# Fused attention and feed-forward: the local value product in fp32 without a split, its joined words in two buffers, and the global jobs at other steps

## The chip, the cores and the metric

The kernel runs on one core of one Trainium2 chip. The metric is the device time of one execution in microseconds; the number that counts is the median of several runs. The core's engines are named as in the profile: PE is TensorE (PEld its weight loads), DVE is VectorE, ACT is ScalarE, POOL is GpSimd, and SP is the engine that issues the transfers (its queue is SPq).

## The reference, cut to what matters

Eight batches of eight heads, 512 local and 32 global positions, head dimension 64. The attention result is laid out as 4608 tokens of 512 and goes through a feed-forward layer with a squared relu.

```
k_all = np.concatenate([k_g, k_l], axis=2)
v_all = np.concatenate([v_g, v_l], axis=2)
s_g = scale * np.matmul(q_g, k_all.transpose(0, 1, 3, 2))
out_g = np.matmul(sm(s_g), v_all)
s_ll = scale * np.matmul(q_l, k_l.transpose(0, 1, 3, 2))
mask = np.abs(pos[:, None] - pos[None, :]) <= window          # window = 32
s_ll = np.where(mask, s_ll, -1000000000.0)
s_lg = scale * np.matmul(q_l, k_g.transpose(0, 1, 3, 2))
a_l = sm(np.concatenate([s_lg, s_ll], axis=-1))
out_l = np.matmul(a_l, np.concatenate([v_g, v_l], axis=2))
...
h = np.maximum(x @ w_in, 0.0)
return (h * h @ w_out).astype(np.float32)
```

Global queries see all 544 keys; a local query sees the 32 global keys and the local keys at most 32 away.

## The kernel before, in words

**Units.** The work is cut into 128 "heads" t: a batch, a half of its 512 local positions (256 queries) and one of eight heads. Eight heads make a group; a group's 256 tokens are one block of the feed-forward layer, which is cut into eight steps m. There are 16 such blocks and a 17th for the global tokens: 136 steps. One loop (line 614) runs both: iteration t works on head t's scores and softmax, on head t−1's product with the values, and on feed-forward step m = t − 9. An iteration is called a step below.

**Precision.** The first 16 heads ("plain") use fp32 matmuls on the raw data. From head 16 on an operand is split into a head, the value rounded to fp32r by a cast on ACT, and a rest, the difference, by a subtraction on DVE; several fast matmuls (head by head, head by rest, rest by head) stand for one in fp32. So split_qk and split_qk_rest (lines 132 and 142) treat q and k, split_v (149) the values, parts and parts_rest (238, 243) the turned probabilities, act2 (495) the hidden values.

**One local head.** load_head (91) loads raw(t): 608 columns of k and q and 192 of values, 400 KB. split_qk takes the heads of q and k into the tile qk, split_qk_rest the rests. scores (155) multiplies into s. softmax1 (172) adds the mask and takes the maximum on DVE into prob, softmax2 (192) takes the exponentials and their sums on ACT, softmax3 (201) the reciprocal and the scaling on DVE. turn (223) copies prob on POOL into planes of 16-bit words and has a DMA transpose turn them into the tile turned; join (231) puts the words together again on POOL in the tile joined. av (250) multiplies with the values into xa, nine matmuls of 128 or 256 moving columns. x_evac (278) takes the result out as x_h and x_l, the operands of the feed-forward layer.

**The feed-forward step.** gemm1 (472), in two halves, multiplies x with the first weights into h; act1 (488) takes relu and square into the PSUM tile pt, act2 the split gh and gl; gemm2 (506), in two halves, adds into the two output tiles o, which evac (528) copies to ot and stores after eight steps.

**Global heads.** Four local heads share a global score tile (g_scores, line 313); its work is spread over later steps as jobs (lines 692 to 711), a step and a place in the step for each: g_load_v and g_split_v for the values, g_soft, g_exp and g_norm for the softmax, g_turn and g_join for the turning (POOL copies and a DMA transpose too), g_parts for the split, g_av for the product gxo (13 matmuls), g_x for the result.

**The order.** From iteration 17 on (FREE, line 33) instructions issued through pe, ve, ac, po and sp stay in the order of the program on their engine; SP's transfers issued through sp are among them: turn's transpose and the loads of raw. An engine executes its instructions in that order, so an instruction that waits holds back all that stand behind it. In one step of the kernel before ACT runs x_evac(t−2), split_v(t), softmax2(t), parts(t−1), split_qk(t+1), act1, act2; SP runs turn(t)'s transpose and then load_head(t+2).

```
        if live and not early:
            softmax3(t)
            turn(t)
        if NPLAIN <= t + 2 < NT:
            load_head(t + 2)
```

The whole code of the functions that the change touches:

Of the kernel before, what the change touches and what calls it, by code (L numbers as in the profile page):

```python
# [7 lines left out]
F32 = mybir.dt.float32  # L8
F32R = mybir.dt.float32r
# [7 lines left out]
DM, DFF = 512, 2048  # L17
P = 128
HALF = 256
NGR = 2 * B  # L20
NT = NGR * H
# [17 lines left out]
def f(ap):  # L39
    return ap.bitcast(F32)  # L40
# [19 lines left out]
def attention_moe(  # L60
# [30 lines left out]
    def load_head(t):  # L91
        if plain(t):
            w_take(1)
            raw = wp.tile([P, 1024], F32, tag="w", name=f"raw{t}")[:, :PK]
        else:
            raw = p2.tile([P, PS], F32, tag="raw", name=f"raw{t}")
        if t == 0:
            nc.sync.dma_start(raw[:, : QC + KC], pk[t, :, : QC + KC])
        else:
            sp.dma_start(raw, pk[t, :, : raw.shape[1]])  # L100
        heads[t] = dict(raw=raw)

    load_head(0)
    con = cp.tile([P, P + 4 * WIN], F32, name="con")
# [15 lines left out]
    prob = cp.tile([P, 2 * WIN], F32, name="prob")  # L120
    planes = cp.tile([P, 1024], U16, name="planes")
    turned = cp.tile([P, 8, P], U16, name="turned")
    joined = cp.tile([P, 512], F32, name="joined")
    ml = cp.tile([P, P], F32R, name="ml")
    nc.gpsimd.memset(planes, 0)
    nc.gpsimd.memset(f(ml), 0.0)
    pt = ps_a.tile([P, 512], F32, name="pt")
    nc.gpsimd.memset(f(qgz), 0.0)
    nc.gpsimd.memset(sg[:, :, 608:], 0.0)
# [12 lines left out]
    def split_qk_rest(t):  # L142
# [2 lines left out]
        raw, hi = heads[t]["raw"], heads[t]["hi"]  # L145
        ve.tensor_sub(hi[64:, :KC], raw[64:, :KC], f(hi[64:, :KC]))
        ve.tensor_sub(hi[:, QK:], raw[:, KC:QK], f(hi[:, KC:QK]))

    def split_v(t):
        raw = heads[t]["raw"]  # L150
        v = heads[t]["v"] = p2.tile([P, 2, 192], F32R, tag="v", name=f"v{t}")
        ac.copy(v[:, 0, :], raw[:, QK:])
        ve.tensor_sub(v[:, 1, :], raw[:, QK:], f(v[:, 0, :]))

    def scores(t):
        hd = heads[t]
# [72 lines left out]
        sp.dma_start_transpose(out=turned, in_=planes)  # L229

    def join(t):
        words = joined.bitcast(U16).rearrange("p (n h) -> p h n", h=2)
        po.tensor_copy(words, turned.rearrange("p (h c) n -> p h (c n)", h=2))

    def sides(z):
        return z.rearrange("p (c n) -> p c n", n=128)[:, 0:4:3, :]

    def parts(t):

        ph = heads[t]["ph"] = p1.tile([P, 512], F32R, tag="ph", name=f"ph{t}")  # L240
        ac.copy(ph, joined)

    def parts_rest(t):
        ph = heads[t]["ph"]
        pl = heads[t]["pl"] = p1.tile([P, 256], F32R, tag="pl", name=f"pl{t}")
        ve.tensor_sub(ph[96:, 128:384], joined[64:96, 128:384], f(ph[64:96, 128:384]))
        ve.tensor_sub(ml[:64, :], joined[:64, 192:320], f(ph[:64, 192:320]))
        ve.tensor_sub(pl.rearrange("p (c n) -> p c n", c=2), sides(joined), sides(f(ph)))

    def av(t):  # L250
        hd = heads[t]
        c = QC + KC
        if plain(t):

            xa = ps_a.tile([P, HALF], F32, tag="xa", name=f"xa{t}")
            v, pts = hd["raw"][:, c:], hd["pts"]
            mm = [
                (xa, v[:, 0:128], pts[:, 256:512]),
                (xa[:, 0:128], v[:, 64:192], pts[:, 0:128]),
                (xa[:, 128:256], v[:, 128:256], pts[:, 128:256]),  # L260
            ]
        else:
            xa = ps_a.tile([64, HALF], F32, tag="xa", name=f"xa{t}")
            v, ph, pl = hd["v"], hd["ph"], hd["pl"]
            mm = []
            for u in range(2):
                o, vs, hs = xa[:, 128 * u : 128 * u + 128], slice(64 * u, 64 * u + 64), slice(384 * u, 384 * u + 128)
                mm += [(o, v[:, 0, vs], ph[:, hs]), (o, v[:, 1, vs], ph[:, hs])]
            mm += [(xa, v[:, i, 128:], ph[:, 128:384]) for i in range(2)]
            mm.append((xa[:, 64:192], v[:, 0, 128:], ml))  # L270
            for u in range(2):
                o, vs, ps = xa[:, 128 * u : 128 * u + 128], slice(64 * u, 64 * u + 64), slice(128 * u, 128 * u + 128)
                mm.append((o, v[:, 0, vs], pl[:, ps]))
        for i, (o, a, b) in enumerate(mm):
            pe.matmul(o, a, b, start=i == 0, stop=i == len(mm) - 1, skip_group_check=True)
        hd["xa"] = xa[:64, :]
# [14 lines left out]
    def g_load(t):  # L291

        b, grp = t // 16, (t // 4) % 2

        def cols(z, j):
            return bass.AP(z.tensor, z.offset + 64 * j, [list(z.ap[0]), [256, 2], [160, 2], [1, 32]])

        src = qg[b, grp].rearrange("p (a b) n -> p a b n", a=2)
        if plain(t):
            qz = p1.tile([P, 512], F32, tag=("ph", "gvl", "gvh", "ph")[t // 4], name=f"qz{t}")  # L300
            nc.gpsimd.memset(qz, 0.0)
            qr = p1.tile([P, 2, 2, 32], F32, tag="qr", name=f"qr{t}")
            (nc.sync if t else nc.scalar).dma_start(qr, src)
            nc.gpsimd.tensor_copy(cols(qz, 0), qr)
        else:
            qz = qgz
            qr = p1.tile([P, 2, 2, 32], F32, tag="qr", name=f"qr{t}")
            nc.sync.dma_start(qr, src)
            ac.copy(cols(qgz, 0), qr)
            ve.tensor_sub(cols(qgz, 1), qr, f(cols(qgz, 0)))  # L310
        state["qz"] = qz
# [215 lines left out]

    def evac(blk, tiles=(0, 1)):
        for i in tiles:
            pool, tag = ((p1, "ptl"), (p1, "gvl"))[i]  # L530
            ot = pool.tile([P, DM], F32, tag=tag, name=f"ot{blk}_{i}")
            ac.copy(ot, moe["o"][i])
            if blk < NGR:
                b, hf = divmod(blk, 2)
                r0 = b * 544 + 32 + hf * 256 + i * P
                nc.sync.dma_start(out[r0 : r0 + P, :], ot)
            else:
                for bb in range(4):
                    r0 = (4 * i + bb) * 544
                    nc.sync.dma_start(out[r0 : r0 + 32, :], ot[32 * bb : 32 * bb + 32, :])  # L540
# [41 lines left out]
    def w_tick(t, place):  # L582
        if t < len(PLAN):
            for c in PLAN[t].split(",")[place]:
                {"b": w_pass, "s": w_chunk}[c]()
# [28 lines left out]
    for t in range(NSTEP + LAG + 1):  # L614
# [11 lines left out]
            transposes(t - 1)  # L626
        if new:
            join(t - 1)
        for job, *args in jobs.pop((t, 6), ()):
            job(*args)  # L630
        if live and not early:
            scores(t)
        if old:
            pt_copy(t - 1)
        if NPLAIN <= t - 2 < NT:
            x_evac(t - 2)
        done = 0 < m <= NSTEP and m % 8 == 1 and m > 8
        if done:
            evac(m // 8 - 1, (0,))
        if live:  # L640
            softmax1(t)
        if run:
            gemm1(m, 0)
        if live and not early:
            split_v(t)
        if live:
            softmax2(t)
        if new:
            parts(t - 1)
        if live and not early:  # L650
            softmax3(t)
            turn(t)
        if NPLAIN <= t + 2 < NT:
            load_head(t + 2)
        for place in (4, 3):
            for job, *args in jobs.pop((t, place), ()):
                job(*args)
        if done:
            evac(m // 8 - 1, (1,))
        w_tick(t, 0)  # L660
        if live and early:
            g_scores(t)
# [5 lines left out]
            g_scores(t)  # L668
        if early and t + 1 < NPLAIN:
            scores(t + 1)  # L670
        if t + 1 < NT and not early:
            split_qk(t + 1)
        if run:
            act1(m)
        if old:
# [4 lines left out]
        w_tick(t, 1)  # L680
        if t + 1 == NPLAIN:
            split_qk(t + 1)
        if new:
            parts_rest(t - 1)
        if t + 1 < NT:
            split_qk_rest(t + 1)
        if live:
# [2 lines left out]
            if t % 4 == 3 and t + 1 < NT:  # L690
                g_load(t + 1)
        if live and t % 4 == 3 and (t // 8) % 2 == 1:
            d = t if t % 8 == 3 else t + 2
            for at, *job in (
                (d, 2, g_load_v, 0),
                (d + 1, 3, g_soft),
                (d + 1, 1, g_exp),
                (d + 2, 3, g_norm),
                (d + 3, 3, g_split_v, 0),
                (d + 3, 2, g_load_v, 1),  # L700
                (d + 3, 6, g_turn),
                (d + 4, 6, g_join),
                (d + 4, 3, g_parts),
                (d + 4, 0, g_av, 0),
                (max(d + 5, 17), 3, g_x, 0),
                (d + 5, 2, g_split_v, 1),
                (max(d + 6, 17), 0, g_av, 1),
                (max(d + 7, 18), 3, g_x, 1),
            ):
                place, job, *args = job  # L710
                jobs.setdefault((at, place), []).append((job, t, *args))
        for job, *args in jobs.pop((t, 2), ()):
            job(*args)
        if m == NSTEP:
            for i in range(2):
# [2 lines left out]
                evac(NBLK - 1, (i,))  # L718
        elif m > 0:
            gemm2(m - 1, 0)  # L720
        for job, *args in jobs.pop((t, 0), ()):
            job(*args)
        if 0 < m < NSTEP:
            gemm2(m - 1, 1)
        if new:
            av(t - 1)
        if run:
            act2(m)
        w_tick(t, 2)
        for job, *args in jobs.pop((t, 1), ()):  # L730
            job(*args)
# [82 lines left out]
```

## Time and profile before

| | |
|---|---|
| median of 3 runs | 1070.35 us (1070.1 to 1071.05) |
| the profiled execution | 1071.19 us, of which 1069.1 us lie between its first and last instruction (the span) |
| mean granted TensorE clock | 0.994 |
| DMA queue of SP and ACT | 126.32 MB, 44.5% of the time of 16 DMA engines |

The profile is that of one execution. A page sums it up; the other views answer questions to its trace. In lists of groups stand: line, engine, operation, out<-in by the tile's names (numbers left out), shapes, how many; then busy microseconds and mean nanoseconds of one; then the idle time of the engine just before and what ended it. Nearly all instructions carry line 53, a helper's, so tiles tell them apart. In the list of waits stand: engine and tile, what it waited for, microseconds in all, how often, the longest. In a timeline: start, duration, engine, operation, how many in one row. Matmuls are pipelined, so one record overlaps the next; what a stream of them costs is read from start to start. One fp32 matmul leaves two records. In the list of transfers the last number is the time from issue to landing.

### The profile page before, as it was taken

How to read it: one execution, taken by the hardware profiler on the slowest of the kernel's cores; microseconds unless marked ns; L12 is line 12 of the kernel's file. 1: busy time of each engine (PE TensorE's matmuls, PEld its weight loads, DVE VectorE, ACT ScalarE, POOL GpSimd, SP SyncE). 2: the span in 40 equal slices, each digit the busy share in tenths (PEclk: the TensorE clock that was granted, in tenths of full speed). 3: DMA queues.
4: the chain of work that ended last, by engine and by line, in shares of the span. 5: the costliest groups of instructions: out<-in, count | busy, mean ns of one | idle time of the engine just before them, and what ended most of it. 6: DMA issues, size and time to landing. Idle time of an engine off the chain costs nothing.

```text
span 1069.1 us, 20564 instructions
## 1 busy us (share of the span) xinstructions
PE 1029.5 (96%) x7040; PEld 902.3 (84%) x7040; DVE 867.7 (81%) x2445; ACT 721.5 (67%) x1743; POOL 385.0 (36%) x544
## 2 busy tenths in 40 slices
PE   8999989999999999999999999999999999999998
PEld 6776778988898888888888889888888888889896
DVE  5689878899989888898979999898989999893311
ACT  6889766767767766767666766776667676664432
POOL 1010344444445343444444443453445353441000
PEclk9999989999999999999999999999999999999999
DMA  9772444445444544454544444545444454341000
GB/s 367 310 258 80 104 103 115 114 116 125 116 123 101 136 103 101 115 118 123 122 115 116 116 120 109 123 104 125 125 110 105 118 135 110 103 95 54 5 21 20
DMA packets 193576, 127.69 MB, mean 119 GB/s; under 512 B 143552, under 2 KB 168640, under 8 KB 193472
## 3 DMA queue, kind: packets, MB, share of 16 engines
q1 hardware_dynamic: 193328, 126.32, 44.5%
q8 instruction: 55, 0.90, 0.4%
q14 instruction: 49, 0.40, 0.1%
q10 hardware_dynamic: 144, 0.07, 0.0%
HBM read 82.84 MB, written 8.91 MB: 86 GB/s over the span
## 4 chain that ended last, share of the span: by engine, by line
PE 43%; DVE 37%; ACT 8%; issue 5%; DMA 3%; POOL 2%; SPq 0%; DVEq 0%; POOLq 0%; ACTq 0%
PE o L53 17%; PE h L53 16%; DVE prob L53 6%; DVE st L53 5%; DVE qk L53 5%; PE xa L53 4%; ACT prob L53 3%; DVE v L53 3%; PE s L53 3%; DVE gl L53 2%; PE gxo L53 2%; DVE x_l L53 2%; DVE ph L53 2%; DVE pl L53 2%; DMA raw<-in_pk_dram 2%
## 5 line engine op out<-in xcount | busy, mean ns | idle before, releaser
L53 PE MATMUL h<-x_h,ws 128*128 128x256 f32 x2048 | 391.4, 284 | 0.0
L53 PEld LDWEIGHTS h<-x_h,ws 128*128 128x128 f32 x2048 | 329.1, 192 | 0.7
L53 PE MATMUL o<-ws,gh 128*128 128x512 f32 x1024 | 324.4, 398 | 3.2 <-ACT ot L53 3.0
L53 PE MATMUL h<-x_l,ws 128*128 128x256 f32 x1024 | 290.9, 284 | 1.1 <-DVE x_l L53 1.1
L53 POOL COPY joined<-turned 128x1024 uint16<-128x1024 uint16 x112 | 155.3, 1387 | 378.1 <-DMA turned<-planes 232.9
L53 POOL COPY planes<-prob 128x448 uint16<-128x448 uint16 x336 | 171.3, 547 | 152.1 <-DVE prob L53 152.1
L53 PEld LDWEIGHTS o<-ws,gh 128*128 128x128 f32 x1024 | 182.5, 189 | 38.2 <-ACT ot L53 7.0
L53 PE MATMUL o<-ws,gl 128*128 128x512 f32 x512 | 202.1, 395 | 0.0
L53 PEld LDWEIGHTS h<-x_l,ws 128*128 128x128 f32 x1024 | 197.0, 192 | 3.2 <-DVE x_l L53 2.6
L53 ACT ACTIVATE prob<-prob,st 128x224 f32<-128x224 f32 x224 | 106.3, 475 | 90.3 <-DVE st L53 89.5
L53 DVE TENSOR_TENSOR gl<-pt,gh 128x512 fp32r<-128x512 f32 x128 | 87.5, 684 | 73.2 <-ACT gh L53 72.0
L53 DVE TENSOR_TENSOR qk<-raw,qk 64x352 fp32r<-64x352 f32 x224 | 109.1, 487 | 8.7 <-ACT qk L53 1.6
L53 PEld LDWEIGHTS o<-ws,gl 128*128 128x128 f32 x512 | 96.3, 188 | 23.1
L53 ACT ACTIVATE pt<-h 128x512 f32<-128x512 f32 x128 | 74.2, 580 | 54.3 <-PE h L53 54.0
L53 ACT CAST x_h<-xa 64x256 fp32r<-64x256 f32 x120 | 43.7, 364 | 98.2 <-PE xa L53 97.9
L53 ACT CAST ph<-joined 128x512 fp32r<-128x512 f32 x112 | 68.9, 615 | 41.2 <-POOL joined L53 39.0
L53 PE MATMUL s<-qk 128*128 128x224 f32 x448 | 83.5, 298 | 8.2 <-DVE qk L53 5.6
L53 DVE TENSOR_SCALAR st<-st 128x2 f32<-128x2 f32 x128 | 62.5, 488 | 34.0 <-ACT prob L53 29.8
L53 ACT CAST qk<-raw 128x608 fp32r<-128x608 f32 x112 | 78.1, 697 | 8.7 <-DMA raw<-in_pk_dram 8.6
L53 DVE TENSOR_TENSOR v<-raw,v 128x192 fp32r<-128x192 f32 x112 | 80.5, 719 | 0.0
L53 DVE CUSTOM_DVE_ANT_0 prob<-s,con 128x224 f32<-128x224 f32 x224 | 77.7, 382 | 3.0 <-PE s L53 1.3
L53 ACT ACTIVATE pt<-pt 128x512 f32<-128x512 f32 x128 | 74.5, 582 | 4.0
(85 smaller groups left out, 1616.9 us busy)
## 6 DMA issues: line engine op xcount, KB each, us to landing
raw<-in_pk_dram SPq DMA_DIRECT2D x112, 400.0 KB, 3.5
wr<-in_w_dram SPq DMA_DIRECT2D x32, 512.0 KB, 8.0
gv<-in_vg_dram SPq DMA_DIRECT2D x32, 320.0 KB, 3.8
out_dram<-ot SPq DMA_DIRECT2D x32, 256.0 KB, 2.4
raw<-in_pk_dram SPq DMA_DIRECT2D x15, 432.0 KB, 8.2
qr<-in_qg_dram SPq DMA_DIRECT2D x31, 64.0 KB, 3.1
turned<-planes SPq DMA_TRANSPOSE x112, 3.1
out_dram<-ot SPq DMA_DIRECT2D x8, 64.0 KB, 1.7
```

The costliest lines, as they stand in the source:

```text
L53: r = method(*args, **kwargs)
```

## The change

The local values and the turned probabilities are no longer split: av multiplies them as they are, in fp32, with three matmuls in place of nine. The functions split_v, parts and parts_rest and their tiles are gone. The values come by a load of their own (load_v, at the start of step t), so that raw holds 608 columns. joined becomes a tile with two buffers, and so does ot. In the loop, evac takes both tiles at one place, split_qk(t+1) stands between softmax1 and softmax2 (in steps with an evac behind softmax2), the jobs of place 6 (g_turn, g_join) stand behind turn, those of place 0 (g_av) ahead of gemm2's first half, av between gemm2's two halves, and x_evac at the end of the same step. The global jobs get another list of steps.

```diff
         else:
-            raw = p2.tile([P, PS], F32, tag="raw", name=f"raw{t}")
+            raw = p2.tile([P, QK], F32, tag="raw", name=f"raw{t}")
...
+    def load_v(t):
+        v = heads[t]["v"] = p2.tile([P, 192], F32, tag="v", name=f"v{t}")
+        sp.dma_start(v, pk[t, :, QK:PS])
...
-    joined = cp.tile([P, 512], F32, name="joined")
-    ml = cp.tile([P, P], F32R, name="ml")
...
-    def split_v(t):
...
     def join(t):
+        joined = heads[t]["pts"] = p2.tile([P, 512], F32, tag="joined", name=f"joined{t}")
         words = joined.bitcast(U16).rearrange("p (n h) -> p h n", h=2)
         po.tensor_copy(words, turned.rearrange("p (h c) n -> p h (c n)", h=2))
-
-    def sides(z):
...
-    def parts(t):
...
-    def parts_rest(t):
...
-            v, ph, pl = hd["v"], hd["ph"], hd["pl"]
...
+            v, pts = hd["v"], hd["pts"]
+            mm = [
+                (xa, v[:, 128:], pts[:, 128:384]),
+                (xa[:, 0:128], v[:, 0:64], pts[:, 0:128]),
+                (xa[:, 128:256], v[:, 64:128], pts[:, 384:512]),
+            ]
...
         for i in tiles:
-            pool, tag = ((p1, "ptl"), (p1, "gvl"))[i]
-            ot = pool.tile([P, DM], F32, tag=tag, name=f"ot{blk}_{i}")
+            ot = p2.tile([P, DM], F32, tag="ot", name=f"ot{blk}_{i}")
...
         if new:
             join(t - 1)
-        for job, *args in jobs.pop((t, 6), ()):
-            job(*args)
         if live and not early:
+            load_v(t)
             scores(t)
         if old:
             pt_copy(t - 1)
-        if NPLAIN <= t - 2 < NT:
-            x_evac(t - 2)
         done = 0 < m <= NSTEP and m % 8 == 1 and m > 8
         if done:
-            evac(m // 8 - 1, (0,))
+            evac(m // 8 - 1)
         if live:
             softmax1(t)
         if run:
             gemm1(m, 0)
-        if live and not early:
-            split_v(t)
+        if t + 1 < NT and not early and not done:
+            split_qk(t + 1)
         if live:
             softmax2(t)
-        if new:
-            parts(t - 1)
+        if t + 1 < NT and not early and done:
+            split_qk(t + 1)
         if live and not early:
             softmax3(t)
             turn(t)
+        for job, *args in jobs.pop((t, 6), ()):
+            job(*args)
         if NPLAIN <= t + 2 < NT:
             load_head(t + 2)
...
-        if done:
-            evac(m // 8 - 1, (1,))
         w_tick(t, 0)
...
-        if t + 1 < NT and not early:
-            split_qk(t + 1)
         if run:
             act1(m)
...
-        if new:
-            parts_rest(t - 1)
         if t + 1 < NT:
             split_qk_rest(t + 1)
...
-            d = t if t % 8 == 3 else t + 2
+            d = t if t % 8 == 3 else t + 1
             for at, *job in (
-                (d, 2, g_load_v, 0),
                 (d + 1, 3, g_soft),
                 (d + 1, 1, g_exp),
                 (d + 2, 3, g_norm),
-                (d + 3, 3, g_split_v, 0),
-                (d + 3, 2, g_load_v, 1),
+                (d + 2, 1, g_load_v, 0),
                 (d + 3, 6, g_turn),
                 (d + 4, 6, g_join),
-                (d + 4, 3, g_parts),
-                (d + 4, 0, g_av, 0),
-                (max(d + 5, 17), 3, g_x, 0),
-                (d + 5, 2, g_split_v, 1),
-                (max(d + 6, 17), 0, g_av, 1),
-                (max(d + 7, 18), 3, g_x, 1),
+                (d + 4, 3, g_split_v, 0),
+                (d + 4, 1, g_load_v, 1),
+                (d + 5, 3, g_parts),
+                (d + 6, 0, g_av, 0),
+                (d + 6, 1, g_split_v, 1),
+                (d + 6, 1, g_x, 0),
+                (d + 7, 0, g_av, 1),
+                (d + 7, 1, g_x, 1),
             ):
...
         elif m > 0:
             gemm2(m - 1, 0)
...
+        if new:
+            av(t - 1)
         if 0 < m < NSTEP:
             gemm2(m - 1, 1)
-        if new:
-            av(t - 1)
         if run:
             act2(m)
+        if new:
+            x_evac(t - 1)
```

More of the change, by code (lines that the diff above doesn't have):

```diff
@@ L122, in attention_moe @@
     turned = cp.tile([P, 8, P], U16, name="turned")
-    joined = cp.tile([P, 512], F32, name="joined")
-    ml = cp.tile([P, P], F32R, name="ml")
     nc.gpsimd.memset(planes, 0)
-    nc.gpsimd.memset(f(ml), 0.0)
     pt = ps_a.tile([P, 512], F32, name="pt")
@@ L147, in split_qk_rest @@
         ve.tensor_sub(hi[:, QK:], raw[:, KC:QK], f(hi[:, KC:QK]))
-    def split_v(t):
[L150 to L153, printed above, removed]
     def scores(t):
@@ L231, in join @@
     def join(t):
+        joined = heads[t]["pts"] = p2.tile([P, 512], F32, tag="joined", name=f"joined{t}")
         words = joined.bitcast(U16).rearrange("p (n h) -> p h n", h=2)
         po.tensor_copy(words, turned.rearrange("p (h c) n -> p h (c n)", h=2))
-    def sides(z):
-        return z.rearrange("p (c n) -> p c n", n=128)[:, 0:4:3, :]
-    def parts(t):
-        ph = heads[t]["ph"] = p1.tile([P, 512], F32R, tag="ph", name=f"ph{t}")
-        ac.copy(ph, joined)
-    def parts_rest(t):
[L244 to L248, printed above, removed]
     def av(t):
@@ L263, in av @@
             xa = ps_a.tile([64, HALF], F32, tag="xa", name=f"xa{t}")
-            v, ph, pl = hd["v"], hd["ph"], hd["pl"]
[L265 to L273, printed above, removed]
+            v, pts = hd["v"], hd["pts"]
[4 more added lines that the diff above has]
+            ]
         for i, (o, a, b) in enumerate(mm):
@@ L299, in g_load @@
         if plain(t):
-            qz = p1.tile([P, 512], F32, tag=("ph", "gvl", "gvh", "ph")[t // 4], name=f"qz{t}")
+            qz = p1.tile([P, 512], F32, tag=("ptl", "gvl", "gvh", "ptl")[t // 4], name=f"qz{t}")
             nc.gpsimd.memset(qz, 0.0)
@@ L652, in attention_moe @@
             turn(t)
+        for job, *args in jobs.pop((t, 6), ()):
+            job(*args)
         if NPLAIN <= t + 2 < NT:
             load_head(t + 2)
-        for place in (4, 3):
-            for job, *args in jobs.pop((t, place), ()):
-                job(*args)
-        if done:
-            evac(m // 8 - 1, (1,))
+        for job, *args in jobs.pop((t, 3), ()):
+            job(*args)
         w_tick(t, 0)
@@ L711, in attention_moe @@
                 jobs.setdefault((at, place), []).append((job, t, *args))
-        for job, *args in jobs.pop((t, 2), ()):
+        for job, *args in jobs.pop((t, 0), ()):
             job(*args)
@@ L720, in attention_moe @@
             gemm2(m - 1, 0)
-        for job, *args in jobs.pop((t, 0), ()):
-            job(*args)
+        if new:
+            av(t - 1)
         if 0 < m < NSTEP:
             gemm2(m - 1, 1)
-        if new:
-            av(t - 1)
         if run:
             act2(m)
+        if new:
+            x_evac(t - 1)
         w_tick(t, 2)
```

## Prediction

> **What bounds the kernel now.** I read the page first (busy time, chain), then the waits of the engines and of SP's queue, then the timeline of one step of the loop.
>
> ```profile
> span 1069.1 us, 20564 instructions
> ...
> PE 1029.5 (96%) x7040; PEld 902.3 (84%) x7040; DVE 867.7 (81%) x2445; ACT 721.5 (67%) x1743; POOL 385.0 (36%) x544
> ...
> PE 43%; DVE 37%; ACT 8%; issue 5%; DMA 3%; POOL 2%; SPq 0%; DVEq 0%; POOLq 0%; ACTq 0%
> ```
>
> ```profile
> PEld s L53 <- DVE qk L53: 16.7, 51, 2.0
> ...
> PEld gxo L53 <- DVE ptl L53: 11.3, 13, 0.9
> ...
> ACT qk L53 <- DMA raw<-in_pk_dram: 8.6, 7, 3.5
> ```
>
> TensorE is nearly full, and when it does stand, it is mostly VectorE that is late (the rests of q and k for the next scores, the rests for the global product). The third row matters below: already now the load of the next head's raw lands so late that ACT waits for it seven times, at the place where the split stands today. How much it stands is read from the step. The first and last scores of the local heads and the matmuls of one step:
>
> ```profile
> L53 PE MATMUL s<-qk x448: 269/274/665, 96.8 to 952.5; 128*128 128x224 f32 x150
> ```
>
> ```profile
> 541.85 2.88 PE h L53 x24
> ```
>
> ```profile
> 599.73 0.63 PE L53 MATMUL o<-ws,gh 128*128 128x512 f32 x2
> ...
> 601.13 0.63 PE L53 MATMUL xa<-ph,v 128*64 128x128 f32 x6
> ...
> 601.78 0.65 PE L53 MATMUL s<-qk 128*128 128x224 f32 x4
> 602.27 0.29 PE L53 MATMUL h<-x_h,ws 128*128 128x256 f32 x1
> ...
> 605.60 0.29 PE L53 MATMUL gs<-qk,qgz 128*128 128x288 f32 x1
> 605.73 0.62 PE L53 MATMUL o<-ws,gh 128*128 128x512 f32 x2
> ...
> 607.11 0.22 PE L53 MATMUL gxo<-gvh,pth 128*64 128x128 f32 x1
> ...
> 607.89 0.44 PE L53 MATMUL o<-ws,gh 128*128 128x512 f32 x1
> ```
>
> Matmuls overlap, so start to start is the price. 448 matmuls at four a head are 112 heads, 111 steps in 952.5 − 96.8 − 0.5 = 855 us: 7.70 us a step. Without waits a step is four s 0.49 (601.78 to 602.27), 24 h 2.88, one gs 0.13, twelve o 2 × 1.40 (599.73 to 601.13), nine xa 0.65: 6.95. The 28 global products in this stretch (13 matmuls, 607.11 to 607.89: 0.78) add 0.20 a step. So 0.55 a step, 61 us in all, is TensorE standing still.
>
> **The change: the product.** Nine split matmuls at 0.65 become three in fp32 over 256, 128 and 128 moving columns. The plain heads run just such a set:
>
> ```profile
> 89.58 1.04 PE L53 MATMUL xa<-pts,raw 128*128 128x256 f32 x6
> 90.46 1.88 PE L53 MATMUL o<-wf,r 128*128 128x512 f32 x4
> ```
>
> Six records, 0.88 start to start. There the stationary side has 128 columns and here 64, which can only make the weight loads shorter, and those run beside the matmuls; the bounds are the 0.65 of now, if fp32 cost nothing more, and the 1.04 to the end of the last record. I take 0.88, since start to start is how the other terms are counted. TensorE's step without waits grows by 0.23 to 7.18, 7.38 with the global products; over 111 steps +26 us if TensorE sets the pace. The Trainium skill (FP8 and Floating Point Precision, TensorE Precision Notes) counts four passes for true fp32. At four times the split price (h: 0.12 us for 256 columns) that would be 0.96 us; the row's 0.88 is a little less, and the measured row is used. By the rule this term would be 9 us larger.
>
> **What it removes.**
>
> ```profile
> L53 ACT CAST ph<-joined 128x512 fp32r<-128x512 f32 x112 | 68.9, 615 | 41.2 <-POOL joined L53 39.0
> L53 DVE TENSOR_TENSOR v<-raw,v 128x192 fp32r<-128x192 f32 x112 | 80.5, 719 | 0.0
> L53 DVE TENSOR_TENSOR ph<-joined,ph 32x256 fp32r<-32x256 f32 x112 | 63.0, 563 | 9.2 <-ACT ph L53 5.8
> ```
>
> These three alone are 0.62 us of ACT and 1.28 us of VectorE a step; the casts of v and the ml and pl rests go too. This is what would end most of the 61 us of waits, if nothing else came in.
>
> **What it moves: the point that decides.** split_qk(t+1), which reads raw(t+1), moves from behind gemm1's second half to ahead of softmax2(t) on ACT, in all steps but those with an eviction. And raw(t+2) is still issued on SP behind turn(t), which waits for the three copies to planes, which wait for softmax2(t). ACT and SP keep program order from step 17 on. So raw(t+1) → split → softmax2(t) → softmax3 → planes → transpose issue → raw(t+2) becomes a ring closed once per step. Before, the split stood behind the softmax, right ahead of act1, and the ring closed over two steps. Behind the waiting split on ACT now stand softmax2, act1, gh and x_h; for them wait VectorE (softmax3, gl, x_l), POOL with its copies, and TensorE, whose next scores need the rests of q and k that VectorE takes after softmax3. That SP does hold the load back, and how long the ring is:
>
> ```profile
> SPq L53 <- POOL planes L53: 439.8, 123, 6.2
> ```
>
> ```profile
> 604.24 0.48 ACT L53 ACTIVATE prob<-prob,st 128x224 f32<-128x224 f32 x1 [1.52 <-DVE st L53]
> ...
> 604.43 0.35 DVE L53 TENSOR_TENSOR v<-raw,v 128x192 fp32r<-128x192 f32 x1
> ...
> 605.09 0.19 ACT L53 ACTIVATION_READ_ACCUMULATOR prob<-prob,st 128x1 f32 x1
> ...
> 605.69 0.70 ACT L53 CAST qk<-raw 128x608 fp32r<-128x608 f32 x1
> ...
> 606.19 1.78 POOL L53 COPY planes<-prob 128x448 uint16<-128x448 uint16 x3 [1.86 <-DVE prob L53]
> ...
> 607.99 1.24 SPq L53 DMA_TRANSPOSE turned<-planes  x1
> ...
> 609.32 0.53 SPq L53 DMA_DIRECT2D raw<-in_pk_dram  x1
> ```
>
> ```profile
> 613.49 1.19 POOL L53 COPY planes<-prob 128x448 uint16<-128x448 uint16 x3 [0.93 <-DVE prob L53]
> ```
>
> ```profile
> L53 POOL COPY joined<-turned 128x1024 uint16<-128x1024 uint16 x112 | 155.3, 1387 | 378.1 <-DMA turned<-planes 232.9
> ...
> raw<-in_pk_dram SPq DMA_DIRECT2D x112, 400.0 KB, 3.5
> ...
> turned<-planes SPq DMA_TRANSPOSE x112, 3.1
> ...
> raw<-in_pk_dram SPq DMA_DIRECT2D x1, 304.0 KB, 3.1
> ```
>
> raw's buffer was free when v's rest ended at 604.78, yet the load went out at 609.32, right behind the transpose: it is SP's order, not the buffer, that times it. The ring: split 0.70; the two exponentials with their sums 1.04 (604.24 to 605.28); reciprocal and scaling until the first copy 0.91 (to 606.19); the copies 1.19 to 1.78, taken as 1.70, since the q and k rests will run on VectorE beside them; to the transpose 0.02; transpose issue to load issue 1.33; landing 3.1 to 3.5, taken as 3.3, since the load shrinks from 400 to 304 KB, the size of the page's other row. Sum 9.0 us, against 7.38 for TensorE and 7.70 now. TensorE is not late in this ring: after scores it has 6.7 us of matmuls to do and waits for the rest of the 9.0, and the product finds its operand ready, as the join ends before the next raw lands (below). Nor are VectorE or ACT: what is left of their work, some 0.6 and 1.3 us a step less than now by the three rows above (on ACT the one, on VectorE the other two), fitted into 7.70.
>
> Two kinds of steps differ. In a step with an eviction (one in eight) softmax2 goes ahead of the split, and the copies wait only for the join before them on POOL. The transpose went out 1.33 before the load, so it has landed 1.33 + 3.3 − 3.1 = 1.5 before raw; the join (1.39) ends 0.1 before raw lands. The copies start there and not 0.70 + 1.04 + 0.91 = 2.65 after it: 2.8 us are saved, 0.35 a step. And g_turn, twice in 16 steps, now follows turn: its copies and its transpose come between turn's transpose and the load.
>
> ```profile
> L53 POOL COPY gp<-sg 128x1088 uint16<-128x1088 uint16 x16 | 19.2, 1198 | 30.3 <-ACT sg L53 30.3
> ...
> L53 POOL COPY gp<-sg 128x64 uint16<-128x64 uint16 x48 | 10.2, 249 | 0.0
> ```
>
> That is 1.20 + 3 × 0.25 = 1.95 of copies and some 1.4 for the issue in place of 1.33: +2.1, 0.26 a step. Period: 9.0 − 0.35 + 0.26 = 8.9 us. 111 × (8.9 − 7.70) = +133 us.
>
> Costed at nothing: the separate v load (one issue of half a microsecond, which stands ahead of turn on SP, in the time that SP waits for the copies anyway; without that cover 0.5 a step); the second buffers of joined and of the evicted tile; x_evac in the same step (TensorE's last six o, 1.40, cover it until the next gemm1); the spread of the global jobs (it takes away waits such as the 11.3 us above, which the ring would hide in any case). After the last head nothing changes. The profiled execution took 1071.19, 2.1 over its span; 1071.2 + 133 = 1204, and the median of the runs, 1070.35, lies 0.8 lower: **1203**. Bounds of the ring: copies 1.19 and landing 3.1 give 8.2 (1126); copies 1.78 and landing 3.5 give 9.2 (1237); landings are longer when other transfers run, so I keep room above.
>
> **Rivals.**
> *The ring does not close* (faster): the smaller raw goes out as soon as its buffer is free and has landed when ACT asks. It decides if the way from raw to raw is under 7.38, which needs the landing 1.6 us shorter than taken, or another order on SP. Then TensorE paces: 111 × 7.38 = 819, with a third of the 61 us of waits left 839, so 16 under 855: 1055. For it: VectorE loses work. Against: the SP row and 604.78 against 609.32. Chance 0.09.
> *Only the fp32 price* (slower): no ring, and the waits stay: +26, 1096. Against it: VectorE is relieved. Chance 0.04.
> *The ring and the clock* (much slower): TensorE now rests 8.9 − 7.18 = 1.7 us a step. Two rests of that length in a row did halve its clock once:
>
> ```profile
> 139.70 0.45 PE L53 MATMUL xa<-ph,v 128*64 128x256 f32 x2 [1.80 <-DVE ph L53]
> ...
> 142.52 1.44 PE L53 MATMUL s<-qk 128*128 128x224 f32 x4 [1.84 <-DVE qk L53]
> ```
>
> ```profile
> 142.00:148.00 6.00, 5.48 (x24) 5.31 (x25) 4.54 (x14) 5.01 (x12) 3.68 (x4) 0.50 0.37 116
> ```
>
> Six microseconds at clock 0.50 cost 3: such a step takes 7.38 + 3 = 10.4. Without a rest in it the clock comes back, so it would alternate with 8.9: mean 9.65, 1070 + 111 × 1.95 = 1287. Against: single rests, 7 us apart. Chance 0.08. The Trainium skill (TensorE: Matmul & The Clock Gate, the table of what matters for your kernels) only forbids rests over about 3 us; by it the clock would hold in ordinary steps.
>
> **How the numbers follow.** The ring as summed has 0.79, its own range 1140 to 1270. The rivals at 1055 and 1096 (0.13) are left out, the clock's is taken in part; range 1140 to 1270. This measurement can tell 0.2%, 2 us, from no change. Faster 0.08 (the first rival, but for a rest), same 0.02, slower 0.90.
>
> **What would show it.** Right: ACT qk waits for DMA raw in most steps (now 7 times), by 1.5 us and more; steps near 8.9; DVE far below 81%; TensorE waits for qk. The product at 0.88. Wrong: steps near 7.4 and no wait for raw.

## The result, and the profile after

The changed kernel takes **1215.08 us** (median of 4 runs, 1213.34 to 1216.68) beside 1070.7 us for the kernel before on the same chip: ratio 1.1349, 95% interval 1.1329 to 1.1368. It is slower, by 144 us.

The page of the changed kernel, busy time and then the chain that ended last:

```profile
span 1211.6 us, 19435 instructions
...
PE 1101.4 (91%) x6704; PEld 913.3 (75%) x6704; DVE 645.9 (53%) x1997; ACT 618.3 (51%) x1519; POOL 400.4 (33%) x543
...
DMA 27%; PE 19%; ACT 16%; DVE 13%; POOL 10%; SPq 8%; issue 7%; POOLq 0%; DVEq 0%; ACTq 0%
DMA raw<-in_pk_dram 26%; POOL planes L53 8%; ACT prob L53 8%; SPq L53 8%; PE o L53 8%; PE h L53 7%; ACT qk L53 5%; DVE prob L53 3%; DVE st L53 3%; DVE qk L53 2%; PE xa L53 2%; POOL gp L53 2%; DMA turned<-planes 1%; PE s L53 1%; DVE gl L53 1%
```

VectorE has lost 222 us of work, as the edit promises, and yet the span has grown. The chain says where: it ran 43% through PE before; now it runs 26% through the loads of raw, and the rest is spread over every engine. No engine is a bound any more. A chain that hops from engine to engine, with none of them in front, fits a ring of dependences. The list of waits names the link at which the ring stands, first for the engines, then for SP's queue:

```profile
ACT qk L53 <- DMA raw<-in_pk_dram: 444.9, 103, 7.2
DVE st L53 <- ACT prob L53: 377.4, 111, 6.9
```

```profile
SPq L53 <- POOL planes L53: 593.5, 112, 7.0
```

ACT's split of q and k waited for raw 7 times and 8.6 us before; now in 103 of 112 heads, 445 us. One turn of the ring in the timeline, from one split to the next:

```profile
602.91 0.70 ACT L53 CAST qk<-raw 128x608 fp32r<-128x608 f32 x1 [4.57 <-DMA raw<-in_pk_dram]
...
603.51 0.48 ACT L53 ACTIVATE prob<-prob,st 128x224 f32<-128x224 f32 x1
...
604.36 0.19 ACT L53 ACTIVATION_READ_ACCUMULATOR prob<-prob,st 128x1 f32 x1
...
605.46 1.68 POOL L53 COPY planes<-prob 128x448 uint16<-128x448 uint16 x3 [2.97 <-DVE prob L53]
...
607.16 1.23 SPq L53 DMA_TRANSPOSE turned<-planes  x1
...
608.45 0.57 SPq L53 DMA_DIRECT2D raw<-in_pk_dram  x1
...
611.77 0.70 ACT L53 CAST qk<-raw 128x608 fp32r<-128x608 f32 x1 [5.12 <-DMA raw<-in_pk_dram]
```

Read it downwards: split 0.60 until the first exponential, exponentials 1.04 (to 604.55), scaling 0.91, copies 1.68 and 0.02, 1.29 between the two issues, 3.32 until the load has landed and the next split starts. That is 8.86 us, and nothing in it is TensorE. The first and last scores give the mean step:

```profile
L53 PE MATMUL s<-qk x448: 264/274/667, 95.2 to 1094.4; 128*128 128x224 f32 x150
```

(1094.4 − 95.2 − 0.5) / 111 = 9.00 us, against 7.70 before: 111 × 1.30 = 144 us, the whole loss. TensorE's single steps scatter widely around this mean, from 7.43 us upwards; the turns of the ring, from split to split, are steadier, 8.2 to 10.9 us where neither an eviction nor g_turn falls into them.

### The profile page after: what moved, and what is told of

Its sections match the earlier page's. It is cut to its first block, busy times and chain, and to the rows that moved or that the text cites. A ratio compares the mean times of both kernels' runs of the same rounds, so it can differ in the third digit from the quotient of the medians.

```text
span 1211.6 us, 19435 instructions
## 1 busy us (share of the span) xinstructions
PE 1101.4 (91%) x6704; PEld 913.3 (75%) x6704; DVE 645.9 (53%) x1997; ACT 618.3 (51%) x1519; POOL 400.4 (33%) x543
## 4 chain that ended last, share of the span: by engine, by line
DMA 27%; PE 19%; ACT 16%; DVE 13%; POOL 10%; SPq 8%; issue 7%; POOLq 0%; DVEq 0%; ACTq 0%
DMA raw<-in_pk_dram 26%; POOL planes L53 8%; ACT prob L53 8%; SPq L53 8%; PE o L53 8%; PE h L53 7%; ACT qk L53 5%; DVE prob L53 3%; DVE st L53 3%; DVE qk L53 2%; PE xa L53 2%; POOL gp L53 2%; DMA turned<-planes 1%; PE s L53 1%; DVE gl L53 1%
## 5 line engine op out<-in xcount | busy, mean ns | idle before, releaser
L53 PE MATMUL h<-x_h,ws 128*128 128x256 f32 x2048 | 405.3, 291 | 0.0
L53 PEld LDWEIGHTS h<-x_h,ws 128*128 128x128 f32 x2048 | 341.9, 199 | 0.8
L53 PE MATMUL o<-ws,gh 128*128 128x512 f32 x1024 | 336.6, 410 | 0.0
L53 POOL COPY planes<-prob 128x448 uint16<-128x448 uint16 x336 | 190.3, 603 | 278.2 <-DVE prob L53 278.2
L53 DVE TENSOR_SCALAR st<-st 128x2 f32<-128x2 f32 x128 | 23.4, 183 | 381.4 <-ACT prob L53 377.4
L53 PEld LDWEIGHTS h<-x_l,ws 128*128 128x128 f32 x1024 | 204.3, 200 | 1.0 <-DVE x_l L53 0.2
L53 PE MATMUL xa<-joined,v 128*64 128x128 f32 (+1 forms) x672 | 120.7, 316 | 37.5 <-POOL planes L53 24.3
L53 PEld LDWEIGHTS xa<-joined,v 128*64 128x64 f32 x672 | 76.5, 136 | 98.1 <-POOL planes L53 33.1
L53 PEld LDWEIGHTS s<-qk 128*128 128x128 f32 x448 | 71.1, 200 | 96.5 <-ACT x_h L53 32.7
L53 DVE TENSOR_TENSOR qk<-raw,qk 64x352 fp32r<-64x352 f32 x224 | 132.4, 591 | 19.5 <-ACT qk L53 13.1
```

Source lines behind the costliest of these rows:

```text
L53: r = method(*args, **kwargs)
```

## The experiments

Two theories stood against each other. The **ring**: the place of split_qk on ACT and that of the load on SP close a ring of dependences once per step. The **price**: the fp32 product, its additional transfers and a lower clock cost the time in any order. All times are medians; each ratio is to the kernel before on the same chip.

**1. The split back at its late place** (all else as changed).

```diff
-        if t + 1 < NT and not early and not done:
-            split_qk(t + 1)
...
-        if t + 1 < NT and not early and done:
-            split_qk(t + 1)
...
+        if t + 1 < NT and not early:
+            split_qk(t + 1)
         if run:
             act1(m)
```

> The changed kernel with one thing put back: split_qk(t+1) stands behind the softmax again, right ahead of act1, in every step. Ring theory (raw, split, softmax2, copies, transpose issue, next raw load, once per step): the ring closes over two steps again, and TensorE sets the pace. The fastest steps of the changed kernel take 7.43 us, with the global products 7.63, against 7.70 a step in the kernel before; with 10 to 20 us of waits left this gives 1060 to 1085 us. Price theory (the fp32 product, its extra transfers and the lower clock are slow in any order): the time stays above 1150. ACT's wait for raw should fall from 445 us to under 30 by the first, and stay by the second.

Measured: 1077.95 us, ratio 1.0077 (1.0062 to 1.0092). The wait for raw:

```profile
ACT qk L53 <- DMA raw<-in_pk_dram: 34.9, 39, 1.8
```

**2. The load ahead of turn's transpose** (the split stays early).

```diff
             load_v(t)
             scores(t)
+        if NPLAIN <= t + 2 < NT:
+            load_head(t + 2)
...
-        if NPLAIN <= t + 2 < NT:
-            load_head(t + 2)
```

> The changed kernel with the ring cut at another link: load_head(t+2) is issued on SP right behind load_v(t), ahead of turn(t)'s transpose; split_qk stays in front of softmax2. Ring theory: the load no longer waits for the copies, raw has landed when ACT asks, and TensorE sets the pace: 1060 to 1085 us, as with the late split. Price theory: above 1150. If only one of the two variants recovers the time, the ring is not the whole cause.

Measured: 1071.79 us, ratio 1.0019 (1.0009 to 1.003). Its busy line, its chain and the wait for raw:

```profile
PE 1055.4 (98%) x6704; PEld 892.2 (83%) x6704; DVE 679.2 (63%) x1997; ACT 634.1 (59%) x1519; POOL 404.9 (38%) x543
...
PE 87%; ACT 5%; DVE 4%; issue 2%; DMA 1%; POOL 1%; SPq 0%; POOLq 0%; ACTq 0%; DVEq 0%
```

```profile
ACT qk L53 <- DMA raw<-in_pk_dram: 9.3, 4, 3.7
```

Two cuts at different links, on different engines, and either gives back nearly all: the ring is shown, and the price theory has fallen. But both end at the time of the kernel before and no lower, with the chain 87% on PE. TensorE is now the bound by itself, and something has made it slower.

**3. The early split alone, in the kernel before.** No fp32 product, no load of its own for v.

```diff
             split_v(t)
+        if t + 1 < NT and not early and not done:
+            split_qk(t + 1)
         if live:
             softmax2(t)
+        if t + 1 < NT and not early and done:
+            split_qk(t + 1)
...
-        if t + 1 < NT and not early:
-            split_qk(t + 1)
         if run:
             act1(m)
```

> The kernel before with this alone: split_qk(t+1) moves between split_v(t) and softmax2(t) (in steps with an eviction behind softmax2). No fp32 product, no load of its own for v. Ring theory: the ring closes once per step here too: split 0.70, exponentials 1.04, scaling 0.91, copies 1.78 (VectorE is busier), 1.33 between the two issues, landing 3.5 for 400 KB: 9.3, less 0.35 for the steps with an eviction, so 111 x (8.9 - 7.7) more than before: about 1205, between 1185 and 1240 us. Price theory: 1065 to 1080, since the product is as before.

Measured: 1213.44 us, ratio 1.1348 (1.1329 to 1.1368): the loss of the whole change, from one moved function. Its chain, ACT's wait for raw and SP's for the copies:

```profile
DMA 31%; DVE 26%; ACT 19%; PE 17%; issue 5%; POOL 0%; SPq 0%; DVEq 0%; POOLq 0%; ACTq 0%
```

```profile
ACT qk L53 <- DMA raw<-in_pk_dram: 276.1, 105, 9.6
```

```profile
SPq L53 <- POOL planes L53: 560.6, 112, 7.9
```

The chain names VectorE where one expects POOL and SP, since a chain follows one releaser at each step, inferred from the times, and VectorE's work on the split product ends at about the moment when the load goes out (the rest ml at 704.46 in one turn, the load at 704.47). The links are those of the ring: in this trace too the load is issued about 1.33 us behind turn's transpose, and the turns without an eviction and without a global transpose take 9.1 us on average. That the time agrees with the changed kernel's within 2 us is chance: here the landing is longer (400 KB, a median of 3.5 us from the load's issue to the next split, against 3.3), there g_turn lies in the ring.

**4. The fp32 product alone, in the kernel before's order** (three fp32 matmuls, load_v, joined in two buffers, as in the diff of the change; order and global jobs as before).

```diff
         if live and not early:
+            load_v(t)
             scores(t)
...
-        if live and not early:
-            split_v(t)
         if live:
             softmax2(t)
-        if new:
-            parts(t - 1)
...
-        if new:
-            parts_rest(t - 1)
```

> The kernel before with the product alone changed: three fp32 matmuls, v by its own load, joined in two buffers, no parts and no split_v; the order of all else and the global jobs as before. Ring theory: no ring, so TensorE's price of the product (0.65 becomes what the changed kernel shows between the neighbouring matmuls, about 1.1: 50 us in all) stands against up to 61 us of waits that the lighter VectorE removes: 1045 to 1085 us. Price theory: 1150 or more.

Measured: 1091.84 us, ratio 1.0216 (1.0191 to 1.024): above my range, below the price theory's. VectorE is as light as in the changed kernel, and TensorE takes 7.45 to 7.47 in an ordinary step, but two steps of 16 still take 9.1 to 12.4, those with the first global product (the second makes it 8.26). Its matmuls wait for their operand:

```profile
PEld gxo L53 <- ACT pth L53: 13.9, 14, 2.6
```

In the old list of jobs g_join, g_parts and this product fall into one step. The variant with the late split, which differs by the new list of jobs, the places of g_turn, av, x_evac and the evictions, and the evicted tiles' buffers, is 14 us faster: that much those moves are worth together here.

**5. The rests ahead of softmax3** (the ring closed; VectorE's two subtractions no longer run beside the copies).

```diff
         if live and not early:
+            if t + 1 < NT and not done:
+                split_qk_rest(t + 1)
             softmax3(t)
             turn(t)
...
-        if t + 1 < NT:
+        if t + 1 < NT and (early or done):
             split_qk_rest(t + 1)
```

> The changed kernel with split_qk_rest(t+1) ahead of softmax3(t) on VectorE (in steps with an eviction at its old place). The ring keeps all its links; only VectorE's two subtractions no longer run beside the three copies to planes. Ring theory: the copies fall from 1.70 towards the 1.19 that they take alone, so 0.35 to 0.5 us less in seven of eight steps: 1166 to 1182 us. If the copies are no link of the ring, or are not slowed by VectorE, the time stays at 1210 to 1220.

Measured: 1181.11 us, ratio 1.1029 (1.1007 to 1.1051). The copies, in the changed kernel and here:

```profile
L53 POOL COPY planes<-prob 128x448 uint16<-128x448 uint16 x336 | 190.3, 603 | 278.2 <-DVE prob L53 278.2
```

```profile
L53 POOL COPY planes<-prob 128x448 uint16<-128x448 uint16 x336 | 157.0, 505 | 297.0 <-DVE prob L53 297.0
```

Three copies a head: 190.3 / 112 = 1.70 us became 157.0 / 112 = 1.40. That is 33 us in all, and the time fell by 34: a microsecond taken from a link of the ring is a microsecond of the kernel, though POOL is busy for a third of the span only.

**6. g_turn back ahead of the scores** (the jobs of place 6 again right behind join).

```diff
             join(t - 1)
+        for job, *args in jobs.pop((t, 6), ()):
+            job(*args)
         if live and not early:
             load_v(t)
...
             turn(t)
-        for job, *args in jobs.pop((t, 6), ()):
-            job(*args)
```

> The changed kernel with the jobs of place 6 (g_turn, g_join) back ahead of the scores, so that the global transpose is issued ahead of turn's and no longer between it and the load of raw. Ring theory: in two of 16 steps the way from turn's transpose to the load falls from about 3.0 to 1.3 us; 0.2 to 0.26 a step, 1186 to 1193 us. Otherwise 1210 to 1220.

Measured: 1190.37 us, ratio 1.1113 (1.1097 to 1.113), 25 us less than the changed kernel. SP's queue in a step with g_turn, in the changed kernel and then in this variant:

```profile
512.57 1.23 SPq L53 DMA_TRANSPOSE turned<-planes  x1
...
514.14 1.31 SPq L53 DMA_TRANSPOSE gq<-gp  x1
...
515.56 0.52 SPq L53 DMA_DIRECT2D raw<-in_pk_dram  x1
```

```profile
646.08 1.32 SPq L53 DMA_TRANSPOSE gq<-gp  x1
647.51 0.52 SPq L53 DMA_DIRECT2D v<-in_pk_dram  x1
648.64 1.24 SPq L53 DMA_TRANSPOSE turned<-planes  x1
649.98 0.52 SPq L53 DMA_DIRECT2D raw<-in_pk_dram  x1
```

From turn's transpose to the load 2.99 us there, 1.34 here. In the changed kernel's trace the 13 turns with a g_turn take 10.72 us on average, the 80 with neither g_turn nor an eviction 9.15: 13 × 1.57 = 20 of the 25 us.

**7. The product twice, with the early load** (to price TensorE's part; the second set of matmuls repeats the first).

```diff
-        for i, (o, a, b) in enumerate(mm):
-            pe.matmul(o, a, b, start=i == 0, stop=i == len(mm) - 1, skip_group_check=True)
+        for _ in range(1 if plain(t) else 2):
+            for i, (o, a, b) in enumerate(mm):
+                pe.matmul(o, a, b, start=i == 0, stop=i == len(mm) - 1, skip_group_check=True)
```

> The changed kernel with the early load (1071.8 us, TensorE paces at 7.43 to 7.46 a step) and the three fp32 matmuls issued twice in a row, the second set starting the sum anew, so that the product is the same. The step grew by 0.48 through the product where the prediction had 0.23. Switch theory: the additional 0.25 is lost at the two borders between split and fp32 matmuls, so a second set costs 0.88: ordinary steps of 8.33 us, about 1170 us. Inherent theory: fp32 matmuls with 64 stationary columns cost 1.1 a set wherever they stand: steps of 8.55 us, about 1194 us.

Measured: 1165.96 us, ratio 1.0888 (1.0871 to 1.0904); ordinary steps of 8.31 to 8.33. TensorE around the product, once (early load) and twice:

```profile
607.57 0.39 PE L53 MATMUL o<-ws,gl 128*128 128x512 f32 x1
607.89 1.08 PE L53 MATMUL xa<-joined,v 128*64 128x256 f32 x6
608.90 0.73 PE L53 MATMUL o<-ws,gh 128*128 128x512 f32 x2
609.47 0.40 PE L53 MATMUL o<-ws,gl 128*128 128x512 f32 x1
```

```profile
606.35 0.39 PE L53 MATMUL o<-ws,gl 128*128 128x512 f32 x1
606.67 1.95 PE L53 MATMUL xa<-joined,v 128*64 128x256 f32 x12
608.55 0.73 PE L53 MATMUL o<-ws,gh 128*128 128x512 f32 x2
```

From start to start the set takes 1.01, and two sets 1.88: the second costs 0.87, the price of the plain heads. The rest belongs to the borders with the split matmuls: 0.14 in the set, and on either side a gap that inner records don't have (607.57 to 607.89 is 0.32 for an o that takes 0.23 elsewhere; the two o behind it take 0.57 where the next two take 0.46). That is 0.34 in all; the four scores, which now follow o, give 0.05 back (610.40 to 610.84 is 0.44 in place of 0.49), so the step grows by 0.87 − 0.65 + 0.34 − 0.05 = 0.51, near the 0.48 to 0.51 measured. The switch theory held: 8.33 forecast for the step, 8.31 measured. The shape (64 stationary columns among 128) is not the reason: the global product, split matmuls of that shape between gs and o in the same trace, follows gs after 0.13 (605.46 to 605.59), as o did in the kernel before, and the two o behind it take 0.50 (606.37 to 606.87). What happens at a border of the two kinds no run shows.

**8. Can both be had: early split and early load in the kernel before.**

```diff
             scores(t)
+        if NPLAIN <= t + 2 < NT:
+            load_head(t + 2)
...
             split_v(t)
+        if t + 1 < NT and not early and not done:
+            split_qk(t + 1)
...
-        if NPLAIN <= t + 2 < NT:
-            load_head(t + 2)
...
-        if t + 1 < NT and not early:
-            split_qk(t + 1)
```

> The kernel before with split_qk(t+1) ahead of softmax2(t) as in the early-split variant and also load_head(t+2) right behind the scores on SP, ahead of turn. The product stays split. Ring theory: without the load behind the transpose there is no ring, so the 143 us that the early split cost vanish; TensorE's step without waits is 6.95, with the global products 7.15, and the rests of q and k come no later than before: 1040 to 1070 us. If the early split itself (ACT's order) were the cost, the time stays above 1150.

Measured: 1105.69 us, ratio 1.0324 (1.0307 to 1.0341), a miss. The ring is open (108 us less than with the early split alone), but SP got a new wait:

```profile
SPq L53 <- POOL planes L53: 351.4, 111, 8.1
SPq L53 <- DVE v L53: 134.0, 72, 4.7
```

There raw still holds the values, so its next load waits until split_v has read them, which SP now meets ahead of the transpose. But TensorE's steps show that this wait is not where the time goes. From the 23rd head on, 93 of 105 steps are as in the kernel before (681.5 us in all, 683.1 before). The other 12, those with the first global product, take 136.7 in place of 115.5 us, and the six steps ahead of all these 15 us more than before. In those 12 the product waits for its operand, here and then in the kernel before:

```profile
PEld gxo L53 <- ACT pth L53: 24.7, 14, 2.9
```

```profile
PEld gxo L53 <- ACT pth L53: 8.0, 13, 1.5
```

Why this operand comes later was not tested; the new order of SP's transfers, among them g_turn's transpose, is a candidate.

**9. The changed order with early load, and the split product in it** (split_v, parts, parts_rest and the nine matmuls put back, with v's own load, joined in one buffer, the evicted tiles in the buffers of ph and gv).

```diff
+        if new:
+            split_v(t - 1)
         if t + 1 < NT and not early and not done:
             split_qk(t + 1)
...
             turn(t)
+        if new:
+            parts(t - 1)
+            parts_rest(t - 1)
...
-        if new:
-            av(t - 1)
         if 0 < m < NSTEP:
             gemm2(m - 1, 1)
+        if new:
+            av(t - 1)
```

> The changed kernel with the early load, and the product of the kernel before in it: split_v(t-1) ahead of split_qk, parts and parts_rest of head t-1 behind turn, nine split matmuls for av at the end of the step, joined in one buffer, the evicted tiles in the buffers of ph and gv. So it has the changed order of loads, splits and global jobs, and TensorE's cheaper product. If the 0.48 us a step that the fp32 product costs TensorE is what keeps the early-load variant (1071.8 us) at the time of the kernel before, TensorE's step falls from 7.45 to 6.95, 54 us in 111 steps, and with 0 to 30 us of new waits for VectorE (it gets 2 us a step back) this gives 1018 to 1050 us, faster than both. If VectorE becomes the bound, 1060 to 1080.

Measured: 1107.81 us, ratio 1.0361 (1.0342 to 1.038), a miss. Its chain and the waits of the scores:

```profile
DVE 41%; PE 33%; ACT 12%; issue 8%; DMA 3%; POOL 1%; DVEq 0%; ACTq 0%; POOLq 0%; SPq 0%
```

```profile
PEld s L53 <- DVE qk L53: 54.1, 104, 3.3
...
PE s L53 <- DVE qk L53: 31.3, 43, 3.2
```

VectorE has its 2 us a step back, and the scores wait for its rests (16.7 and 5.6 us in the kernel before).

**10. The same with the rests of q and k ahead of softmax3.**

```diff
         if live and not early:
+            if t + 1 < NT and not done:
+                split_qk_rest(t + 1)
             softmax3(t)
             turn(t)
...
-        if t + 1 < NT:
+        if t + 1 < NT and (early or done):
             split_qk_rest(t + 1)
```

> The variant with the early load and the split product (1107.8 us), with split_qk_rest(t+1) ahead of softmax3(t) on VectorE as in the experiment on the copies. There the scores waited 85 us for these rests (54 on the weight loads, 31 on the matmuls), and VectorE stood 43 us waiting for the exponentials ahead of softmax3, where the rests now go. If VectorE's order was what held TensorE, most of the 85 us goes: 1030 to 1065 us, faster than both kernels. If VectorE's amount of work (80% busy, and slowed by POOL's copies) is the bound, the waits turn up at the product instead, 1085 to 1110.

Measured: 1085.71 us, ratio 1.0151 (1.0127 to 1.0175). The scores' waits fell to 9.3 and 2.9 us, but the time by 22 only, at the lower edge of the branch in which VectorE's amount of work is the bound: the chain now runs 27% through DVE, 27% through PE and 19% through ACT. No version beat the kernel before; the best of the new order, the early load, equals it within 0.2%.

## Why the prediction was right, point by point

**The direction and the place.** Right: the ring of raw, split, softmax2, softmax3, copies, transpose issue and load, closed once per step. Experiments 1 and 2 open it at two links, experiment 3 makes it without the rest of the change.

**The links.** Forecast 0.70, 1.04, 0.91, 1.70, 0.02, 1.33 and 3.3, in all 9.0; in the turn shown 0.60 (the first exponential starts before the split's record ends), 1.04, 0.91, 1.68, 0.02, 1.29 and 3.32: 8.86. The copies' 1.70, chosen between 1.19 and 1.78 because the q and k rests would run beside them, is the mean measured, and experiment 5 shows that these rests are the reason for part of it.

**The step.** Forecast 8.9, measured 9.00: +144 us in place of +133, and 1215 in place of 1203. The term for g_turn, 0.26 a step or 29 us (its parts as shown add up to 2.0 a turn and not 2.1), measured 25 in experiment 6. The turns of the changed kernel's trace from 116 to 1082 us show the rest: the 80 with neither g_turn nor an eviction took 9.15 on average where 9.0 was forecast, of it 3.48 from the load's issue to the next split in place of 3.3 (+12 us); the 14 in which softmax2 goes ahead of the split took 6.72 in place of 6.2 (+7); the 13 with g_turn 10.72 in place of 11.1 (−5).

**What went as said off the ring.** VectorE became lighter as said, 868 to 646 us busy; v's load and x_evac in the same step, costed at nothing, show no cost in the turns of the ring.

**The term that was wrong.** "TensorE's step without waits grows by 0.23 to 7.18." It grows by 0.48, to 7.43 (the fastest steps of the changed kernel, and the ordinary ones with the early load, 7.43 to 7.46). The price of a set, 0.88, was taken from a stage in which every matmul is fp32, so that row held no border between fp32 and split matmuls; experiment 7 has the set at 0.87 and the rest at the borders. Under the ring the error is hidden, since TensorE waits there anyway. It decides what an open ring is worth: the first rival was priced at 1055, and with the ring open the kernel takes 1072 to 1078, because 111 × 0.48 = 53 us of dearer product meet the 61 us of waits, and the lighter VectorE does not remove all of these: with the early load the scores give 7.75 us a step (95.5 to 956.3), some 12 us in all above the ordinary steps with the global products. So the edit as such gains nothing in the orders tried here.

**The clock.** The rival with the clock was right in part: the mean granted clock fell from 0.994 to 0.975, some 60 us of the span at half clock (2 × 0.025 × 1211.6). It hardly lengthens the ring: in all 93 turns without an eviction the first exponential starts 0.60 to 0.61 us behind the split, so ACT did not wait there for scores, and 103 of 112 splits waited for raw. No link of these turns is TensorE's. What the clock costs in the other turns was not separated.

## What to carry to other kernels

Before an instruction is moved earlier in an engine's order, follow what it waits for back to where that is issued: if the issue stands behind something that depends on the instruction's own successors, the move closes a ring, and its length, not any engine's load, becomes the step. Here the ring showed in the profile as a chain with no engine in front and one long wait repeated in nearly every step; cut it at the cheapest link (here one load moved ahead of one transpose, 143 us). And a duration taken from a stage where all neighbours are of the same kind leaves out what the change of kind costs, here 0.25 us a step.

## What the runs showed of the hardware that was not expected

**Borders between fp32 and split matmuls.** A set of three fp32 matmuls among matmuls on split operands costs TensorE some 0.3 us more than the 0.87 us that a second set behind it costs (0.34 by the rows of experiment 7, 0.25 by the step).

**The clock after one short rest.** Against the clock rival the prediction set that the Trainium skill (TensorE: Matmul & The Clock Gate, the table of what matters for your kernels) forbids only rests over about 3 us. The trace differs: in the changed kernel the clock fell after one rest that the timeline puts at 1.85 us. TensorE there, then busy time and clock (the column behind POOL) in the 3.4 us of that rest and the 3.4 us after it:

```profile
283.02 1.04 PE L53 MATMUL s<-qk 128*128 128x224 f32 x4 [1.85 <-DVE qk L53]
```

```profile
280.90:284.30 3.40, 1.45 (x10) 1.02 (x9) 3.29 (x7) 1.84 (x4) 3.28 (x4) 1.00 0.00 0
284.30:287.70 3.40, 3.40 (x19) 3.40 (x18) 0.87 (x5) 0.00 (x0) 0.61 (x1) 0.51 1.25 128
```

TensorE was busy for 1.45 of 3.40 us, and the clock was 0.51 in the next 3.4. The measurement decides: a rest of less than 2 us can be followed by half the clock. It need not be, as two stretches of the changed kernel show, and less idle time can do it too, as two of the kernel before show:

```profile
683.70:687.11 3.41, 1.50 (x8) 0.90 (x6) 1.77 (x7) 3.33 (x10) 1.04 (x3) 1.00 0.00 0
687.11:690.52 3.41, 3.35 (x20) 2.79 (x21) 3.32 (x8) 2.69 (x7) 0.16 (x1) 1.00 0.60 100
```

```profile
390.85:394.27 3.42, 1.80 (x15) 1.15 (x14) 2.94 (x5) 2.46 (x5) 2.78 (x4) 1.00 0.03 7
394.27:397.68 3.41, 3.41 (x16) 2.72 (x15) 2.74 (x7) 1.39 (x4) 0.51 (x1) 0.50 0.75 171
```

Busy for 1.50 us, TensorE kept its clock; busy for 1.80, it lost half. So the busy time as the profile counts it does not decide alone, and what does stays open.
